# Sliding-window attention and a multiplicative feed-forward on one core: the first phase laid out anew

## The chip, the core and the metric

The kernel runs on one core of one Trainium2 chip. The core has five engines with instruction queues of their own: TensorE (PE, matrix products; PEld is its loading of weights), VectorE (DVE), ScalarE (ACT), GpSimd (POOL) and SyncE (SP). Transfers are issued by an engine's queue and carried out by 16 DMA engines. The metric is the time of one execution on the device in microseconds (us); less is better.

## What is computed

```python
# q, k, v: (8 batches, 8 heads, 576 tokens, 64); w1, w2: (512, 1024); w3: (1024, 1024); w_out: (1024, 512)
scores = scale * np.matmul(q, k.transpose(0, 1, 3, 2))
mask = (rel >= 0) & (rel < 64)                 # a token sees itself and the 63 before it
attn = softmax(np.where(mask, scores, -1e9))
x = (attn @ v).transpose(0, 2, 1, 3).reshape(4608, 512)
out = ((x @ w1) * (x @ w2)) @ w3 @ w_out       # float32, (4608, 512)
```

Inputs and output are float32. The kernel multiplies in float16 and sums in float32.

## The kernel before

**The fold.** There is no nonlinearity between `w3` and `w_out`, so the kernel makes `wc = w3 @ w_out` once (1024 x 512, `wc_sb`) and uses that for all tokens. `w3` is taken in eight row blocks of 128. `fold_t(fc)` transposes block `fc` with eight TensorE instructions (L432) and copies it from PSUM to `w3T` (L434). `fold_mm(fc, c0, c1)` multiplies it with columns `c0:c1` of `w_out` in eight products (L439) and casts the result into `wc_sb` (L440). `load_w3(fc, n)` loads `n` row blocks (L425), `load_wo` a half of `w_out` (L410); both are issued by POOL, and cast from float32 to float16 on the way. `load_rows` and `cast_rows` (a block of `w3` loaded as float32, and then cast by an engine) are defined but not called. The blocks of `w3` lie in space that `ab` and `xT` use later. `load_rows` puts its block into the space of `w2_sb`.

**Attention.** A step `s` covers 256 tokens in four groups of 64. `scores(s)` makes 64 small products (L275) on 32 of the 128 rows at a time; `weigh(d)` takes exp on ScalarE (L284) and applies the band, either by one VectorE product with a mask (L288) or by two selects on POOL (L245, L247). A step that holds a batch's first group always goes to VectorE, whatever `weigh` is told. `values(s)` makes the sums (L301) and the weighted values (L307), and `norm(s)` divides: ln and exp on ScalarE (L317, L318), two VectorE products into `xT` (L320). `keep_sums(s)` stores the sums for a check at the end, by SP. Before that, `load_qk` loads Q or K of a batch in four POOL transfers, one for each pair of heads (L210), and `transposes` turns them in blocks of 32 x 32 on VectorE, one instruction for each half of the heads (L220). `load_v` loads V in blocks of 64 tokens (L230), and `copy_v` makes the shifted copies on VectorE (L236, L238).

**Feed-forward.** A group `g` is 512 tokens. `ffn_ab(g, fc)` makes one 128-column block of `x @ w1` and `x @ w2` with four products each (L367), copies the first by ScalarE (L370) and multiplies on VectorE (L371). `ffn_o(g, t)` makes one output tile of 128 tokens with eight products (L383), and copies it out of PSUM (L385) for `store()`, which hands it to SP (L392). `ffn_ab` can also take two column blocks for half of the tokens (`nf`, `lo`, `hi`); before, no call does. The PSUM tiles of all of these but attention come from one ring of four (`f_ps`), those of attention from a ring of two (`a_ps`).

**Order.** Nothing is scheduled by a planner here (`tc.manual_schedule()`): each engine runs its instructions in the order of the calls in the text, and the framework adds the semaphore waits. POOL has at most eight transfers under way: each new one waits for the one eight before it to land. The text has two parts. The first phase, written out call by call, holds the fold, steps 0 to 6 of attention and groups 0 and 1. It is followed by a loop over groups 2 to 8, where `tick` interleaves attention steps at fixed places. `keep_busy(n)` makes `n` dummy products of the identity (L464).

The first phase of before begins so:

```python
load_qk(0, 'q')
make_identity(nc, ident16)
load_qk(0, 'k')
keep_busy(140)
load_w3(2, 2)
transposes(0, 'k', 1)
...
load_w3(0, 2)
load_wo(0, 256)
fold_t(0, act_cp)
fold_t(2, act_cp)
load_wo(256, 512)
```

Of the kernel before, what the change touches and what calls it, by code (L numbers as in the profile page):

```python
# [9 lines left out]
FP16 = mybir.dt.float16  # L10
I32 = mybir.dt.int32
# [4 lines left out]
P = 128  # L16
# [123 lines left out]
def kernel(  # L140
# [64 lines left out]
    def load_qk(b, which, *js):  # L205

        src = k if which == "k" else q
        r = RUN[b]
        for j in js or range(NJ):
            nc.gpsimd.dma_start(  # L210
                out=t16_of(b, which)[32 * j:32 * j + 32].rearrange("p hh (i n) -> p (hh i) n", n=r * D),
                in_=src[b, 2 * j:2 * j + 2].rearrange("hh (i p r) d -> p (hh i) (r d)", p=32, r=r))

    def transposes(b, which, hh):

        dst = kTs if which == "k" else qTs
        r = RUN[b]
        if b not in dst:
            dst[b] = sb.tile([P, 2, S, 2], FP16, name=which + "T")
        nc.vector.transpose(  # L220
            dst[b][:, hh].rearrange("q t c -> q (t c)").bitcast(I32).rearrange("q (i p r) -> q i r p", p=32, r=r),
            t16s[which, b][:, hh].bitcast(I32).rearrange("p (i r e) -> p i r e", r=r, e=32))
# [9 lines left out]
    def copy_v(b, half, i0, i1):  # L232

        vh = v16s[b % 3].rearrange("p (i o) h d -> p i o (h d)", o=2)
        if half == 0:
            dve_cp(vh[0:D, i0:i1, 1], vh[D:P, i0:i1, 0])  # L236
        else:
            dve_cp(vh[D:P, i0:i1, 1], vh[0:D, i0 + 1:i1 + 1, 0])  # L238
# [135 lines left out]
    def ffn_o(g, t, cp=dve_cp):  # L374
# [5 lines left out]
        for c0, c1, cp in halves:  # L380
# [4 lines left out]
            cp(o_sb[:, c0:c1], o_ps[:, 0:c1 - c0])  # L385
            stores.append((r0, c0, c1, o_sb))

    def store():
        while stores:
            r0, c0, c1, o_sb = stores.pop(0)  # L390
            queue = nc.scalar if c1 - c0 < DM and c0 == 0 else nc.sync
            queue.dma_start(out=out[r0:r0 + P, c0:c1], in_=o_sb[:, c0:c1])  # L392
# [34 lines left out]
    def fold_t(fc, cp):  # L427
# [5 lines left out]
        w3Ts[fc] = sb.tile([P, 8, P], FP16, name="w3T", bufs=4)  # L433
# [40 lines left out]
    load_qk(0, 'q')  # L474
    make_identity(nc, ident16)
    load_qk(0, 'k')
    keep_busy(140)
    load_w3(2, 2)
    transposes(0, 'k', 1)
    transposes(0, 'k', 0)  # L480
    transposes(0, 'q', 0)
    make_ones(nc.vector)
    load_w3(0, 2)
    load_wo(0, 256)
    fold_t(0, act_cp)
    fold_t(2, act_cp)
    load_wo(256, 512)
    transposes(0, 'q', 1)
    load_w3(4, 2)
    fold_t(1, dve_cp)  # L490
    load_v(0, 0, 2, 4)
    fold_t(3, dve_cp)
    make_band()
    load_v(0, 6, 7)
    scores(0)
    load_w3(6, 2)
    load_w12(1, 0, 512)
    fold_mm(3, 0, 256, dve_cp)
    fold_mm(0, 0, 256, act_cp)
    fold_mm(1, 0, 256, dve_cp)  # L500
    load_w12(0, 0, 512)
    weigh(0, nc.vector)
    weigh(1, nc.gpsimd)
    fold_mm(2, 0, 256, dve_cp)
    load_w12(0, 512, 1024)
    fold_mm(0, 256, DM, act_cp)
    fold_mm(2, 256, DM, dve_cp)
    fold_mm(1, 256, DM, act_cp)
    fold_t(4, dve_cp)
    copy_v(0, 0, 0, 2)  # L510
    copy_v(0, 1, 0, 2)
    fold_t(5, act_cp)
    copy_v(0, 0, 2, 4)
    scores(1)
    weigh(2, nc.vector)
    weigh(3, nc.gpsimd)
    fold_mm(4, 0, DM, act_cp)
    fold_mm(3, 256, DM, act_cp)
    load_qk(1, 'k')
    copy_v(0, 1, 2, 3)  # L520
    values(0)
    norm(0)
    load_w12(1, 512, 1024)
    fold_mm(5, 0, DM, dve_cp)
    fold_t(6, act_cp)
    load_qk(1, 'q')
    fold_t(7, dve_cp)
    values(1)
    norm(1)
    fold_mm(6, 0, DM, dve_cp)  # L530
    fold_mm(7, 0, DM, act_cp)
    ffn_ab(0, 2)
    ffn_ab(0, 0)
    ffn_ab(0, 1)
    transposes(1, 'k', 0)
    keep_sums(0)
    load_v(1, 0, 2, 4, 6, 7)
    load_qk(2, 'k')
    transposes(1, 'k', 1)
    ffn_ab(0, 3)  # L540
    ffn_ab(0, 5)
    ffn_ab(0, 4)
    transposes(1, 'q', 0)
# [3 lines left out]
    copy_v(1, 1, 0, 3)  # L547
    copy_v(1, 0, 0, 4)
    scores(2)
    weigh(4, nc.vector)  # L550
    weigh(5, nc.gpsimd)
    ffn_o(0, 0, act_cp)
    load_qk(2, 'q')
    scores(3)
    weigh(7, nc.vector)
    store()
    keep_sums(1)
    ffn_o(0, 1, dve_cp)
    load_v(2, 6, 7)
    weigh(6, nc.gpsimd)  # L560
    values(2)
    norm(2)
    load_v(2, 0, 2, 4)
    store()
    load_qk(3, 'q')
    ffn_o(0, 2, act_cp)
    values(3)
    transposes(2, 'k', 0)
    store()
    norm(3)  # L570
    transposes(2, 'k', 1)
    transposes(2, 'q', 0)
    ffn_o(0, 3, act_cp)
    ffn_ab(1, 0)
    store()
    ffn_ab(1, 1)
    load_qk(3, 'k')
    transposes(2, 'q', 1)
    ffn_ab(1, 2)
    copy_v(2, 0, 0, 4)  # L580
    ffn_ab(1, 3)
    scores(4)
    keep_sums(2)
    weigh(8, nc.vector)
    ffn_ab(1, 4)
    keep_sums(3)
    weigh(9, nc.gpsimd)
    store()
    store()
    store()  # L590
    ffn_ab(1, 5)
    transposes(3, 'q', 1)
    copy_v(2, 1, 0, 3)
    transposes(3, 'q', 0)
    load_v(3, 0, 2, 4)
    load_v(3, 6, 7)
    scores(5)
    weigh(10, nc.gpsimd)
    weigh(11, nc.gpsimd)
    ffn_ab(1, 6)  # L600
    ffn_ab(1, 7)
    values(4)
    store()
    store()
    transposes(3, 'k', 0)
    norm(4)
    store()
    transposes(3, 'k', 1)
    ffn_o(1, 0, act_cp)
    store()  # L610
    load_qk(4, 'k')
    load_qk(4, 'q')
    ffn_o(1, 1, act_cp)
    load_v(4, 0, 2, 4)
    store()
    copy_v(3, 0, 0, 4)
    scores(6)
    weigh(12, nc.vector)
    weigh(13, nc.vector)
    ffn_o(1, 2, dve_cp)  # L620
    keep_sums(4)
    values(5)
    norm(5)
    store()
    load_v(4, 6, 7)
    ffn_o(1, 3, dve_cp)
    copy_v(3, 1, 0, 3)
    keep_sums(5)
# [63 lines left out]
```

## Time and profile before

| | us |
|---|---|
| median of three runs | 259.8 (259.2 to 261.9) |
| the profiled execution | 260.8 |
| its span, first to last instruction | 259.1 |
| TensorE busy | 245.3 |
| of that, dummy products (L464) | 10.2 |

A profile is one execution. In the page's 40 slices a digit is the busy share in tenths, and one slice is 6.5 us. In a row of the timeline stand the start, the time taken, the engine, line and operation, output and input, the count and, in brackets, how long the engine had been idle and what ended that. Rows merge instructions of one kind. The largest groups are the products of the feed-forward:

```profile
L367 PE MATMUL f_ps<-xT,w_sb 128*128 128x512 f16 x576 | 129.6, 379 | 1.1 <-DVE t2k L385 1.1
L383 PE MATMUL f_ps<-wc_sb,ab 128*128 128x512 f16 (+1 forms) x296 | 65.6, 374 | 0.0
```

The first number behind the bar is the time that the group covers, the second the mean of one instruction in ns; products overlap, so 576 of 379 ns cover 129.6 us.

### The profile page before, as it was taken

The numbers are of one execution on the slowest core, as the hardware profiler recorded it, in microseconds if no ns is written. First come the engines' busy times: TensorE is split into PE (matmuls) and PEld (weight loads), VectorE is DVE, ScalarE is ACT, GpSimd is POOL, SyncE is SP. The second block draws the span as 40 slices with busy tenths as digits, with TensorE's granted clock in tenths as the row PEclk, the third lists the DMA queues.
The fourth block names the chain that finished last, engine by engine and source line by source line (L and its number), as shares of the span: only waits on it lengthen the run. The fifth ranks groups of instructions, "written<-read, shape, count | busy, mean of one in ns | idle before, by whom it ended". The sixth has DMA issues, their size and how long they took to land.

```text
span 259.1 us, 8273 instructions
## 1 busy us (share of the span) xinstructions
PE 245.3 (95%) x3622; PEld 129.8 (50%) x3622; DVE 145.8 (56%) x215; ACT 116.3 (45%) x174; POOL 114.3 (44%) x154
## 2 busy tenths in 40 slices
PE   2959999999999899999999999999999999999992
PEld 2958654454445345544444444444554444444441
DVE  0065664887877746656755776576466344434421
ACT  1024744276385464546545453654465545234210
POOL 7962867659669678593089018003000303003000
PEclk9999999999999999999999999999999999999999
DMA  5999999999994999599449909900300120022022
GB/s 80 170 201 189 194 205 206 155 198 149 186 159 53 188 203 150 83 140 213 53 66 219 157 0 128 132 5 13 152 3 5 71 100 1 3 81 85 1 79 89
DMA packets 75497, 29.57 MB, mean 114 GB/s; under 512 B 62456, under 2 KB 69880, under 8 KB 75456
## 3 DMA queue, kind: packets, MB, share of 16 engines
q0 software_dynamic: 69984, 19.41, 73.6%
q1 hardware_dynamic: 5328, 9.46, 9.9%
q8 instruction: 29, 0.48, 0.8%
q10 hardware_dynamic: 144, 0.13, 0.1%
q14 instruction: 12, 0.10, 0.1%
HBM read 38.80 MB, written 9.44 MB: 186 GB/s over the span
## 4 chain that ended last, share of the span: by engine, by line
PE 89%; DMA 4%; POOL 2%; ACT 1%; DVE 1%; issue 1%; POOLq 0%
PE f_ps L367 49%; PE f_ps L383 23%; PE f_ps L439 6%; PE a_ps L275 4%; DMA ab<-in_moe_w_dram 4%; PE a_ps L307 3%; PE a_ps L301 2%; PE f_ps L432 1%; POOL k L210 1%; POOL q L210 1%; ACT pt L284 1%; DVE w3T L434 1%; DVE t2k L385 0%; DVE xT L320 0%; POOL ab L425 0%
## 5 line engine op out<-in xcount | busy, mean ns | idle before, releaser
L367 PE MATMUL f_ps<-xT,w_sb 128*128 128x512 f16 x576 | 129.6, 379 | 1.1 <-DVE t2k L385 1.1
L367 PEld LDWEIGHTS <-w_sb 128*128 128x128 f16 x576 | 54.7, 98 | 65.8 <-issue 2.2
L371 DVE TENSOR_TENSOR ab<-f_ps,a_sb 128x512 f16<-128x512 f32 x72 | 49.7, 690 | 41.6 <-PE f_ps L367 39.6
L383 PE MATMUL f_ps<-wc_sb,ab 128*128 128x512 f16 (+1 forms) x296 | 65.6, 374 | 0.0
L370 ACT COPY a_sb<-f_ps 128x512 f32<-128x512 f32 x72 | 42.3, 587 | 48.6 <-PE f_ps L367 48.6
L245 POOL TENSOR_SCALAR_AFFINE_SELECT pt<-pt 128x1024 f16<-128x1024 f16 x11 | 12.6, 1144 | 80.8 <-ACT pt L284 80.7
L383 PEld LDWEIGHTS <-ab 128*128 128x128 f16 x296 | 27.9, 98 | 31.0
L284 ACT ACTIVATE pt<-a_ps 128x1024 f16<-128x1024 f32 x36 | 36.3, 1026 | 13.3 <-PE a_ps L275 13.2
L320 DVE TENSOR_TENSOR xT<-a_ps,r 128x512 f16<-128x512 f32 x36 | 23.2, 687 | 25.7 <-ACT r L318 25.7
L230 POOL DMA_DIRECT2D v<-in_v_dram x40 | 34.0, 863 | 7.1 <-DMA k<-in_k_dram 3.5
L385 ACT COPY t2k<-f_ps 128x512 f32<-128x512 f32 (+1 forms) x19 | 10.9, 575 | 42.3 <-PE f_ps L383 42.3
L288 DVE TENSOR_TENSOR pt<-pt,band 128x1024 f16<-128x1024 f16 x25 | 17.2, 693 | 14.1 <-ACT pt L284 14.0
L210 POOL DMA_DIRECT2D q<-in_q_dram x32 | 20.0, 638 | 4.8 <-DMA w_sb<-in_moe_w_dram 1.4
L220 DVE STREAM_TRANSPOSE kT<-k 128x576 int32<-128x576 int32 x16 | 14.7, 936 | 12.5 <-DMA k<-in_k_dram 12.5
L210 POOL DMA_DIRECT2D k<-in_k_dram x32 | 20.0, 645 | 2.8 <-DMA q<-in_q_dram 0.8
L385 DVE COPY t2k<-f_ps 128x512 f32<-128x512 f32 (+1 forms) x18 | 12.1, 673 | 7.9 <-PE f_ps L383 7.8
L439 PE MATMUL f_ps<-ab,w3T 128*128 128x256 f16 (+1 forms) x96 | 14.6, 308 | 0.3 <-DVE w3T L434 0.3
L220 DVE STREAM_TRANSPOSE qT<-q 128x576 int32<-128x576 int32 x16 | 14.6, 930 | 0.0
L464 PE MATMUL f_ps<-ident 128*128 128x128 f16 x140 | 10.2, 249 | 4.6 <-POOL ident masks.py:199 4.6
L307 PE MATMUL a_ps<-pt,v 128*32 128x64 f16 x1152 | 14.0, 193 | 0.0
L275 PEld LDWEIGHTS <-kT 32*128 32x128 f16 x1152 | 10.4, 92 | 7.2 <-issue 7.0
L317 ACT ACTIVATE ln_s<-a_ps 128x512 f32<-128x512 f32 x18 | 10.8, 597 | 7.2 <-PE a_ps L301 7.2
(43 smaller groups left out, 135.2 us busy)
## 6 DMA issues: line engine op xcount, KB each, us to landing
out_dram<-t2k SPq DMA_DIRECT2D x35, 256.0 KB, 2.5
q<-in_q_dram POOLq DMA_DIRECT2D x32, 144.0 KB, 6.8
k<-in_k_dram POOLq DMA_DIRECT2D x32, 144.0 KB, 7.4
v<-in_v_dram POOLq DMA_DIRECT2D x32, 128.0 KB, 6.1
w_sb<-in_moe_w_dram POOLq DMA_DIRECT2D x8, 256.0 KB, 9.0
ab<-in_moe_w_dram POOLq DMA_DIRECT2D x2, 512.0 KB, 9.1
ab<-in_moe_w_out_dram POOLq DMA_DIRECT2D x2, 512.0 KB, 12.8
xT<-in_moe_w_dram POOLq DMA_DIRECT2D x2, 512.0 KB, 14.1
```

The lines of the kernel that those rows point to most:

```text
L210: nc.gpsimd.dma_start(out=t16_of(b, which)[32 * j:32 * j + 32].rearrange("p hh (i n) -> p (hh i) n", n=r * D), in_=src[b, 2 * j:2 * j + 2] ...
L220: nc.vector.transpose(dst[b][:, hh].rearrange("q t c -> q (t c)").bitcast(I32).rearrange("q (i p r) -> q i r p", p=32, r=r), t16s[which, b ...
L230: nc.gpsimd.dma_start(out=vh[lo:P, c], in_=v[b, :, s0:s0 + P - lo, :].rearrange("h s d -> s h d"))
L284: nc.scalar.activation(pt, held.pop(d).rearrange("k j (a n) -> k (j a) n", a=2), AF.Exp, bias=-SHIFT, scale=scale)
L307: nc.tensor.matmul(o_ps[jp][32 * h:32 * h + 32, 0, o0:o0 + 64], v16s[b % 3][:, max(0, t - 1), 4 * jp + h, x:D:2], pt[:, h, 64 * i:64 * i + ...
L320: nc.vector.tensor_tensor(xT[:, 2 * jp:2 * jp + 2, x0:x0 + W], o_ps[jp][:, 0].rearrange("p (x n) -> p x n", x=2), r[:, jp].unsqueeze(1).br ...
L367: nc.tensor.matmul(d[:, f * n:f * n + n], w[:, dc, (fc + f) * P:(fc + f + 1) * P], xT[:, dc, x0:x0 + n], start=(dc == 0), stop=(dc == 3), ...
L370: act_cp(a_sb[:, 0:nf * n], a_ps[:, 0:nf * n])
L371: nc.vector.tensor_tensor(ab[:, fc:fc + nf, lo:hi], b_ps[:, 0:nf * n].rearrange("p (f n) -> p f n", f=nf), a_sb[:, 0:nf * n].rearrange("p ...
L383: nc.tensor.matmul(o_ps[:, 0:c1 - c0], ab[:, fc, t * P:t * P + P], wc_sb[:, fc, c0:c1], start=(fc == 0), stop=(fc == 7))
L385: cp(o_sb[:, c0:c1], o_ps[:, 0:c1 - c0])
L439: nc.tensor.matmul(o_ps[:, c0:c1], w3Ts[fc][:, ec, :], wo16[:, ec, c0:c1], start=(ec == 0), stop=(ec == 7))
```

## The change

- Two row blocks of `w3` (0 and 1) are loaded as float32 by SP, and cast by VectorE (three halves) and ScalarE (one). POOL's first loads are half of `w_out` and `w3` blocks 2 and 3, and Q and K of batch 0 come behind the rest of `w_out`.
- In batches with nine tokens to a partition (0 to 2), `load_qk` takes its four parts by half of the tokens and half of the heads, and `transposes` can take one half of the tokens. Batch 0 uses that.
- `w1` and `w2` come as two quarters and a half each. `ffn_ab` for the first four column blocks of group 0 runs in four calls of two blocks and 256 tokens.
- The fold's products all run in halves of 256 columns, `w3T` has eight buffers, and 30 and 20 dummy products take the place of 140.
- The rest of the first phase is reordered. Its last part now has `values(5)` and `norm(5)` ahead of three of the four `ffn_o` of group 1. V block 7 of batch 0 is loaded behind K of batch 2.
- The second half of the very last tile is copied in two pieces, by ScalarE and VectorE, and stored in two.

The loop over groups 2 to 8 is as before.

```diff
-    def load_qk(b, which, *js):
+    def load_qk(b, which, *parts):
...
+        for c in parts or range(4):
+            if r == 9:
+                i, hh = divmod(c, 2)
+                nc.gpsimd.dma_start(
+                    out=t16[:, hh, r * D * i:r * D * (i + 1)],
+                    in_=src[b, hh:H:2, 32 * r * i:32 * r * (i + 1)].rearrange("j (p r) d -> j p (r d)", r=r))
...
-    def transposes(b, which, hh):
+    def transposes(b, which, hh, *halves):
...
+        for t0, t1 in [(S // 2 * i, S // 2 * (i + 1)) for i in halves] or [(0, S)]:
...
+            if c0 == 0:
+                cp(o_sb[:, c0:c1], o_ps[:, 0:c1 - c0])
+                stores.append((r0, c0, c1, o_sb))
+            else:
+                for h0, h1, hcp in ((c0, 384, act_cp), (384, DM, dve_cp)):
+                    hcp(o_sb[:, h0:h1], o_ps[:, h0 - c0:h1 - c0])
+                    stores.append((r0, h0, h1, o_sb))
...
-            queue = nc.scalar if c1 - c0 < DM and c0 == 0 else nc.sync
+            queue = nc.scalar if c1 - c0 < DM and c1 < DM else nc.sync
...
-        w3Ts[fc] = sb.tile([P, 8, P], FP16, name="w3T", bufs=4)
+        w3Ts[fc] = sb.tile([P, 8, P], FP16, name="w3T", bufs=8)
```

The first phase of the changed kernel, up to the end of group 0's `ffn_ab`:

```python
load_rows(0, nc.sync)
load_wo(0, 256)
load_w3(2, 2)
make_identity(nc, ident16)
cast_rows(0, 0, dve_cp)
make_band()
load_w3(4, 2)
keep_busy(30)
load_wo(256, 512)
load_qk(0, 'k', 1); load_qk(0, 'k', 0); load_qk(0, 'q', 1); load_qk(0, 'q', 0)
load_rows(1, nc.sync)
cast_rows(1, 0, dve_cp); cast_rows(0, 1, dve_cp)
fold_t(0, dve_cp); fold_t(2, act_cp)
load_v(0, 0); load_w3(6, 2); load_v(0, 6); load_v(0, 2); load_qk(0, 'k', 2)
cast_rows(1, 1, act_cp)
load_qk(0, 'q', 2)
fold_mm(0, 0, 256, dve_cp)
load_qk(0, 'k', 3); load_w12(0, 256, 512)
fold_t(1, dve_cp)
load_v(0, 4)
fold_t(4, act_cp)
load_qk(0, 'q', 3)
fold_t(5, act_cp)
keep_busy(20)
load_w12(0, 0, 256)
make_ones(nc.vector)
fold_t(3, dve_cp)
transposes(0, 'k', 1, 0)
fold_mm(1, 0, 256, dve_cp)
load_w12(1, 0, 256); load_w12(1, 256, 512); load_qk(1, 'k')
load_w12(0, 512, 1024); load_w12(1, 512, 1024); load_qk(1, 'q')
transposes(0, 'k', 0, 0)
fold_mm(2, 256, DM, act_cp)
transposes(0, 'q', 0, 0); transposes(0, 'q', 1, 0)
fold_mm(3, 256, DM, dve_cp); fold_mm(4, 0, 256, act_cp)
fold_mm(5, 0, 256, act_cp); fold_mm(3, 0, 256, dve_cp)
copy_v(0, 0, 0, 1)
scores(0)
...
scores(1)
weigh(2, nc.vector)
fold_mm(7, 0, 256, act_cp)
copy_v(0, 1, 1, 3)
weigh(3, nc.vector)
ffn_ab(0, 0, 2, 0, 256)
values(1)
norm(1)
keep_sums(0)
fold_mm(4, 256, DM, act_cp)
ffn_ab(0, 2, 2, 0, 256)
load_qk(2, 'k')
transposes(1, 'k', 1)
ffn_ab(0, 0, 2, 256, 512)
ffn_ab(0, 2, 2, 256, 512)
load_v(0, 7)
transposes(1, 'k', 0)
ffn_ab(0, 5)
...
```

And its end, ahead of the loop:

```python
ffn_ab(1, 7)
store()
values(4); norm(4)
load_v(4, 6, 7)
ffn_o(1, 0, act_cp)
transposes(3, 'k', 0)
load_qk(4, 'k'); load_v(4, 0, 2, 4)
store()
values(5); norm(5); keep_sums(4)
ffn_o(1, 1, act_cp)
store()
transposes(3, 'k', 1)
ffn_o(1, 2, dve_cp)
keep_sums(5)
scores(6)
store()
copy_v(3, 0, 0, 4); copy_v(3, 1, 0, 3)
weigh(13, nc.vector); weigh(12, nc.gpsimd)
ffn_o(1, 3, act_cp)
```

More of the change, by code (lines that the diff above doesn't have):

```diff
@@ L514 @@
+    fold_t(7, dve_cp)
+    transposes(0, 'k', 0, 1)
+    values(0)
+    transposes(0, 'k', 1, 1)
+    load_v(1, 0, 2)
+    transposes(0, 'q', 0, 1)
+    norm(0)
+    transposes(0, 'q', 1, 1)
+    load_v(1, 4, 6, 7)
+    fold_mm(7, 256, DM, act_cp)
+    fold_mm(2, 0, 256, dve_cp)
+    fold_mm(6, 0, 256, act_cp)
+    copy_v(0, 0, 3, 4)
+    fold_mm(6, 256, DM, act_cp)
+    copy_v(0, 0, 1, 3)
     scores(1)
     weigh(2, nc.vector)
[L516 to L518 removed]
```

215 lines of the change are left out of this document (103 added, 112 removed).

## The prediction

> **What bounds the kernel now.** I read the page first: shares, then the 40 slices.
>
> ```profile
> PE 245.3 (95%) x3622; PEld 129.8 (50%) x3622; DVE 145.8 (56%) x215; ACT 116.3 (45%) x174; POOL 114.3 (44%) x154
> PE   2959999999999899999999999999999999999992
> DMA  5999999999994999599449909900300120022022
> ```
>
> TensorE is full in nearly every slice, but slices 0 to 2 (a slice is 6.5 us) hold dummy products, and there the DMA engines are full instead. So the trace's start comes next: three rows of the timeline, then the busy time by stage (busy us of PE, weight loads, VectorE, ScalarE and POOL with their instructions, the clock, the DMA share, and GB/s).
>
> ```profile
> 1.49 2.44 POOL L210 DMA_DIRECT2D q<-in_q_dram  x4 [0.96 <-POOLq L676]
> 4.57 10.20 PE L464 MATMUL f_ps<-ident 128*128 128x128 f16 x140 [4.57 <-POOL ident masks.py:199]
> 17.37 1.96 PE L432 MATMUL f_ps<-ident,ab 128*128 128x128 f16 x32 [2.60 <-DMA ab<-in_moe_w_dram]
> ...
> 3.20:12.40 9.20, 7.83 (x101) 7.84 (x102) 0.00 (x0) 0.00 (x0) 8.66 (x15) 1.00 1.07 161
> 12.40:45.60 33.20, 30.28 (x508) 21.02 (x506) 20.05 (x30) 14.92 (x22) 20.77 (x31) 1.00 1.37 199
> 17.37:53.06 35.69, 35.37 (x560) 22.34 (x561) 21.96 (x33) 17.27 (x26) 22.12 (x33) 1.00 1.48 190
> 53.06:89.87 36.81, 35.67 (x683) 17.58 (x675) 28.58 (x41) 21.95 (x31) 27.95 (x35) 1.00 1.36 154
> ```
>
> The 140 products of line 464 are dummies. Useful work begins at 17.37 us, when the first rows of w3 land behind all of Q and K of batch 0. From there to 53.06 TensorE is busy 35.37 of 35.69 us, and 35.67 of 36.81 up to 89.87. So time can be won in three places alone: before 17.37, in the one gap that the last stretch hides, and after the last product. DMA begins at 3.2 us (slice 0 is half full, and the first stage is cut there) and moves 161 GB/s at first, then 199. Transfers, not engines, decide when the weights are there.
>
> **Step 1: useful work starts earlier.** The first work that has to wait for much is now the transpose of rows 2 (`fold_t(2)`). Ahead of it stand two rows of w3 as fp32 by SP, half of w_out and one pair of w3. The sizes are in the page's list of DMA issues, SP's rate in its list of queues.
>
> ```profile
> q1 hardware_dynamic: 5328, 9.46, 9.9%
> ...
> q<-in_q_dram POOLq DMA_DIRECT2D x32, 144.0 KB, 6.8
> v<-in_v_dram POOLq DMA_DIRECT2D x32, 128.0 KB, 6.1
> w_sb<-in_moe_w_dram POOLq DMA_DIRECT2D x8, 256.0 KB, 9.0
> ab<-in_moe_w_dram POOLq DMA_DIRECT2D x2, 512.0 KB, 9.1
> ab<-in_moe_w_out_dram POOLq DMA_DIRECT2D x2, 512.0 KB, 12.8
> ```
>
> The fp32 rows are a kind of load that before doesn't have. SP's queue moved 9.46 MB of stores in 9.9% of the span, 25.7 us, so 369 GB/s; 1.05 MB then takes 2.8 us. The other two are 512 KB each, 1.05 MB: 5.3 us at 199 GB/s, 6.5 at 161. The first bytes of before came at 3.2 us, 1.7 after POOL began to issue; SP's may come at 2.0. Sum: 10.1 to 12.5 us; I take 11.3. By the Trainium skill (DMA: Bandwidth & Descriptors, Issuing engines are not separate DMA queues) a transfer from SP runs on the same 16 engines and saves issue time alone. No run here shows SP and POOL loading together, and the sum above adds the two transfers rather than overlapping them, as that rule would.
>
> The four casts (three on VectorE, one on ScalarE) have no row. A 256-column copy took 423 ns and a 1024-column fp16 one 686 (quoted below), so 0.3 to 0.7 us each: VectorE is through by about 8 us, hidden by the wait for rows 2. Without that cover they would cost 1.5 us. The identity was ready at 4.57 behind four issues (2.44 us in all); now two stand ahead of it. `make_band` stands in POOL's queue next, ahead of the third load:
>
> ```profile
> 14.27 0.66 POOL L245 TENSOR_SCALAR_AFFINE_SELECT band<-band 128x512 f16<-128x512 f16 x1
> ```
>
> That is the largest of its five instructions, so 3.3 us at most: the third load is issued by 7.9, while the two before it are under way to 11.3. No loss. Two waits are new: w2's pieces wait on POOL for the casts, which read the fp32 rows out of w2's buffer, and everything POOL issues later queues behind that. The last cast stands behind one ScalarE copy after rows 2, so it is done near 13, and POOL comes there after 20: nothing. SP has nothing else until the first `keep_sums`.
>
> **Step 2: TensorE's work up to `ffn_ab(0, 5)`, the first block that needs the upper half of w1 and w2.**
>
> ```profile
> 20.27 6.29 PE f_ps L439 x56
> 26.55 0.89 PE f_ps L432 x16
> ...
> 30.77 0.22 PE a_ps L301 x4
> 30.99 0.24 PE a_ps L307 x32
> 31.23 0.11 PE a_ps L301 x4
> ...
> 38.70 13.81 PE f_ps L367 x64
> 52.51 0.70 PE a_ps L275 x62
> ...
> L434 DVE COPY w3T<-f_ps 128x1024 f16<-128x1024 f16 x4 | 2.7, 686 | 2.9 <-PE f_ps L432 2.9
> L440 DVE CAST wc_sb<-f_ps 128x256 f16<-128x256 f32 x4 | 1.7, 423 | 2.7 <-PE f_ps L439 2.7
> ```
>
> The fence has pieces of the chain (start, us), then two groups by line. From 11.3: seven transposes of rows, 0.45 each (16 instructions in 0.89), 3.1; sixteen half products of the fold, 0.90 each (56 in 6.29, eight in one), 14.4; two scores, 0.70, 1.4; two values, 0.81 (0.22 + 0.24 and 0.11 + 0.24), 1.6; four half-token blocks of 16 products of 256 columns at 0.112, 7.2. Before did the same work with 512 columns, so splitting costs 0.3. Twenty dummies add 1.1. Together 28.8: 40.1 us at full clock.
>
> The clock is a term of its own, for the 140 dummies shrink to 30.
>
> ```profile
> 5.00:9.00 4.00, 4.00 (x40) 4.00 (x39) 1.00 1.04 148
> 10.00:14.00 4.00, 4.00 (x76) 4.00 (x74) 1.00 1.11 195
> ```
>
> These are the dummies alone: 40 in 4 us at first, 76 later, so TensorE ran at half speed for 4.4 us at least (to 9.0) and 5.4 at most; I use 4.7. If it does so again from 11.3, that loses 2.35; if the 30 dummies suffice, none. I take 1.2: 41.3.
>
> Do the data keep up? At 199 GB/s from 11.3: w3 rows 4 and 5 at 13.9, the rest of w_out 16.6, the first half of Q and K 19.5, its second half 29.1, the lower half of w1 and w2 33.0. TensorE comes to them at about 14, 17, 22, 31 and 32 to 36. Q and K still have to pass VectorE:
>
> ```profile
> 12.52 2.27 DVE L220 STREAM_TRANSPOSE kT<-k 128x576 int32<-128x576 int32 x2 [12.52 <-DMA k<-in_k_dram]
> ```
>
> Two whole ones in 2.27, so a half takes 0.57, and four stand in a row. VectorE is busy 22 of 36 us there, so it fits, with a margin of a microsecond. `weigh(3)` moves from POOL to VectorE, one multiplication of some 0.7 us; the deeper ring of transposed rows (8 for 4) costs no instruction.
>
> **Step 3: the upper half of w1 and w2.** Behind the lower half stand K of batch 1 (576 KB) and four weight pieces of 256 KB: 5.96 MB since 11.3. At 199 GB/s they are in at 41.3, at 190 (the row of 17.37 to 53.06) at 42.7. I take 42.7, the rate of the stretch with the same mix. It is later than TensorE's 41.3, so the weights decide. Four blocks follow at 1.73 (eight products each, 64 in 13.81) and one scores step, 0.70: 7.6, so 50.3 us. Before, the same point is 52.51 + 0.70 = 53.2. Gain 2.9.
>
> **Step 4: the gap before the regular phase.**
>
> ```profile
> 87.48 1.29 DVE L320 TENSOR_TENSOR xT<-a_ps,r 128x512 f16<-128x512 f32 x2 [0.35 <-ACT r L318]
> 88.22 0.59 PE L367 MATMUL f_ps<-xT,w_sb 128*128 128x512 f16 x2
> 88.68 0.68 DVE L385 COPY t2k<-f_ps 128x512 f32<-128x512 f32 x1
> 89.87 1.46 PE L367 MATMUL f_ps<-xT,w_sb 128*128 128x512 f16 x6 [1.06 <-DVE t2k L385]
> ```
>
> `values(5)` and `norm(5)` end just as block 0 of group 2 wants their output, one product group later. The change puts two output tiles, scores and a third tile in between, 3 x 1.8 + 0.7 = 6.1 us (a tile, like a block, is eight 512-column products), where ln, exp and two multiplications take 2.5. The idle 1.1 us goes. What is late next is `values(5)` itself, which waits for two selects on POOL:
>
> ```profile
> 74.57 0.61 PE a_ps L275 x61
> ...
> 79.87 1.15 POOL L247 TENSOR_SCALAR_AFFINE_SELECT pt<-pt 128x1024 f16<-128x1024 f16 x1
> ```
>
> Before, the second was done 5.8 us after its scores ended (81.0 against 75.2); now two blocks, `values(4)` and one tile lie between, 6.1 us. It just fits, so I count 1.1, between 0 and 1.2. The POOL queue in front of these selects holds only loads whose buffers come free in time. In phase 2 the other moves trade places among engines with a fifth or more of idle time: nothing. `load_v(0, 7)` now stands behind K of batch 2; by the same rate it lands near 53 (1.84 MB after 42.7: Q and V of batch 1, K of batch 2, the piece), and `values(2)` wants it near 55 (50.3, two tiles, one scores).
>
> **Step 5: the end.**
>
> ```profile
> 253.12 0.37 ACT L385 COPY t2k<-f_ps 128x256 f32<-128x256 f32 x1 [2.01 <-PE f_ps L383]
> 253.52 0.38 ACTq L392 DMA_DIRECT2D out_dram<-t2k  x1
> 253.99 0.42 DVE L385 COPY t2k<-f_ps 128x256 f32<-128x256 f32 x1 [1.05 <-PE f_ps L383]
> ```
>
> The last copy is halved over two engines, at most 0.2 less; but ScalarE's first store (253.52) now queues behind its second copy, and a second store of 0.38 behind it. Between -0.2 and +0.4; I take 0.
>
> **Sum.** 2.9 + 1.1 + 0 = 4.0 us. The profiled execution took 260.8 us with a span of 259.1: 256.8 and 255.1. The median of the three runs shown is 259.8, 1.0 lower than the profiled one: 255.8.
>
> **Rivals.** First: the transfers were the bound all along, and a new order moves no byte sooner.
>
> ```profile
> 37.69 0.70 POOL L405 DMA_DIRECT2D w_sb<-in_moe_w_dram  x1 [0.58 <-DMA w_sb<-in_moe_w_dram]
> ...
> DMA to landing us min/median/max: 7.7/9.0/10.6
> ```
>
> Before, the last weights landed at 37.69 + 7.7 = 45.4 at the earliest, with the same bytes ahead of them but 64 KB of V. At that pace the four blocks start at 45.1, the point is 52.7, the gain 0.5 + 1.1: 258.2. For it: DMA is full from 3.2 us on in both. Against: 161 GB/s was the rate for Q and K at the start, and SP starts sooner. With the gap moved rather than gone it is 259.3. Chance 0.23.
>
> Second, slower: the half clock stays. Before, it ended after 4.7 us without a break. Now 30 dummies and one transpose are followed by some 3 us of waiting for rows 2, and the work after them stops again for each load. If it stays at half speed up to `scores(0)`, 9.7 us of work takes 19.4; less the 1.2 counted and the 1.4 by which TensorE was early, +7.1: 262.9. It decides the sign once half speed lasts over 13 us or so after 11.3. Against it: from 11.3 there are no long gaps, and cold work fills them. The Trainium skill (TensorE: Matmul & The Clock Gate, Part 1) has the clock halved by an idle window of about 3.4 us and restored by a busy one; by that the loss would be 1.7 to 3.4 and this rival would fail. The trace agrees as far as its 4.7 us. Chance 0.12, and 0.05 for another new wait of that size.
>
> Third, better: loads run at 199 from 2.0 us and the clock is up. TensorE is ready at 38.9, the weights at 40.1, the point 47.7: 5.5 + 1.1 less, 253.2. Chance 0.12.
>
> **Numbers.** The forecast has 0.48: 255.8, on its own 254.5 to 257.2. The runs of before spread by 1% (259.2 to 261.9), so 1% (257.2 and 262.4) is about what a measurement can tell. Faster 0.60 (forecast and third), same 0.23, slower 0.17. The range leaves out the slow side and the end of the fast one: 253.2 to 260.5.
>
> **What would show it.** Right: first transposes of rows 2 at 10 to 12.5 us; `ffn_ab(0, 5)` starting at 41 to 44 after a wait for w2; ffn_o of group 0 near 50; no idle before group 2; the regular phase unchanged. Wrong: weights landing after 45, 128-column products at 107 ns beyond 20 us, `values` waiting for POOL, or a scores step waiting for VectorE's transposes.

## The result, and the profile after

The changed kernel takes 268.97 us (median of 6 runs, 268.1 to 271.49) against 260.74 of the kernel before on the same chip: ratio 1.034, 95% interval 1.0303 to 1.0377. It is slower by 8.2 us where 4 us less were forecast. The profiled execution took 268.31 us with a span of 266.6, 7.5 more than before. Medians take in every run of a kernel; the ratios leave out the few runs in a slower state (one each of a2, a4 and d1 below, two of d2, the profiled ones of d1 and d2 among them).

The slices of the page of after come first, then the one row of before that was not shown yet (GB/s in the same slices).

```profile
PE   4399988698999799999999999999999999999992
PEclk9769999999999799999999999999999999999999
DMA  6999999999999899949909971900220030022013
GB/s 185 199 181 146 165 127 163 176 131 141 209 195 157 89 183 197 91 79 201 153 1 148 212 73 44 204 6 2 81 82 1 27 138 5 1 81 80 2 57 108
```

```profile
GB/s 80 170 201 189 194 205 206 155 198 149 186 159 53 188 203 150 83 140 213 53 66 219 157 0 128 132 5 13 152 3 5 71 100 1 3 81 85 1 79 89
```

The DMA digits are nines in both, so by the busy share nothing has changed. The bytes have: 146, 165 and 127 GB/s in slices 3 to 5 (20 to 40 us), where before moved 189 to 205 (in 19 to 39). A busy DMA engine is not one that moves much. The same by stage, after first and then before (columns as in the prediction's stages; the last is GB/s):

```profile
18.00:24.00 6.00, 6.00 (x66) 5.36 (x64) 2.62 (x5) 1.71 (x4) 2.29 (x4) 1.00 1.92 162
24.00:36.00 12.00, 10.86 (x281) 8.93 (x279) 8.97 (x19) 6.12 (x12) 9.25 (x13) 1.00 1.45 155
36.00:44.00 8.00, 8.00 (x139) 7.03 (x137) 4.39 (x7) 5.24 (x9) 5.77 (x9) 1.00 1.04 119
```

```profile
18.00:24.00 6.00, 5.68 (x123) 5.09 (x121) 2.51 (x5) 3.70 (x5) 1.72 (x3) 1.00 1.37 202
24.00:36.00 12.00, 12.00 (x293) 8.74 (x291) 8.29 (x14) 8.09 (x13) 8.02 (x11) 1.00 1.56 191
36.00:44.00 8.00, 8.00 (x39) 3.64 (x38) 3.29 (x6) 2.54 (x5) 5.14 (x8) 1.00 1.23 204
```

From 18 to 44 us before moves 1212 + 2292 + 1632 KB (rate by length), 5.14 MB, and after 972 + 1860 + 952, 3.78 MB: 1.35 MB less, 6.8 us of transfers at 199 GB/s. Where TensorE pays for it stands in its timeline of after:

```profile
12.19 1.04 PE L447 MATMUL f_ps<-ident,ab 128*128 128x128 f16 x8 [4.43 <-DMA ab<-in_moe_w_dram]
...
46.41 0.61 PE L377 MATMUL f_ps<-xT,w_sb 128*128 128x512 f16 x2 [0.85 <-DMA w_sb<-in_moe_w_dram]
47.67 0.61 PE L377 MATMUL f_ps<-xT,w_sb 128*128 128x512 f16 x2 [0.65 <-DMA w_sb<-in_moe_w_dram]
48.96 0.60 PE L377 MATMUL f_ps<-xT,w_sb 128*128 128x512 f16 x2 [0.69 <-DMA w_sb<-in_moe_w_dram]
50.34 4.92 PE L377 MATMUL f_ps<-xT,w_sb 128*128 128x512 f16 x22 [0.77 <-DMA w_sb<-in_moe_w_dram]
...
56.54 0.68 PE L285 MATMUL a_ps<-qT,kT 32*128 32x64 f16 x64
...
63.10 0.42 PE L317 MATMUL a_ps<-pt,v 128*32 128x64 f16 x32 [1.11 <-DMA v<-in_v_dram]
...
89.12 0.40 PE L311 MATMUL a_ps<-pt,ones 128*32 128x256 f16 x4 [1.19 <-POOL pt L257]
...
98.92 0.68 PE L285 MATMUL a_ps<-qT,kT 32*128 32x64 f16 x64
```

Rows of w3 start the work at 12.19. Four times TensorE then waits for a piece of the upper halves of w1 and w2, from 45.6 (46.41 less 0.85) to 50.3; `values(2)` waits for V block 7, `values(5)` for POOL's selects. `scores(2)` starts at 56.54 and `scores(7)` at 98.92. In before they start thus:

```profile
52.45 0.68 PE L275 MATMUL a_ps<-qT,kT 32*128 32x64 f16 x64
...
91.26 0.68 PE L275 MATMUL a_ps<-qT,kT 32*128 32x64 f16 x64
```

So 4.1 us are lost by `scores(2)` and 3.6 more by `scores(7)`; from there on both kernels run alike (7.7 there, 7.5 at the end). Part of the 3.6 is the clock. It falls to half behind the wait for POOL, from 89.14 to 92.55 us by the trace's clock records (the 7 in slice 13 of PEclk), and 16 output products take 1.4 us longer there than later on:

```profile
89.95 4.86 PE f_ps L393 x16
...
113.44 3.45 PE f_ps L393 x16
```

The chain of waits of after names the transfers:

```profile
23.98 8.12 DMA k<-in_k_dram
...
36.20 9.39 DMA k<-in_k_dram
```

One load of 144 KB takes 9.39 us from issue to landing (the longest of any K load in before took 8.4), and POOL, which may have eight under way, stands behind it. That time counts the loads ahead as well, and so tells little by itself: b1 below, whose K loads have the form of before, has one of 10.4. The sign is the rate. These are the loads whose form the diff changed: 128 rows of SBUF at a time, four heads outermost at the source, where before had 32 rows of two heads.

### The profile page after: what moved, and what is told of

Read it like the earlier page. It is cut to its first block, busy times and chain, and to the rows that moved or that the text cites. A ratio compares the mean times of both kernels' runs of the same rounds, so it can differ in the third digit from the quotient of the medians.

```text
span 266.6 us, 8234 instructions
## 1 busy us (share of the span) xinstructions
PE 246.0 (92%) x3596; PEld 132.8 (50%) x3596; DVE 145.8 (55%) x223; ACT 118.6 (44%) x181; POOL 118.3 (44%) x155
## 4 chain that ended last, share of the span: by engine, by line
PE 65%; DMA 19%; POOL 12%; issue 2%; DVE 0%; ACT 0%; POOLq 0%
PE f_ps L377 37%; PE f_ps L393 21%; DMA k<-in_k_dram 12%; DMA v<-in_v_dram 7%; PE a_ps L285 3%; POOL v L240 3%; PE a_ps L317 2%; POOL q L213 2%; PE a_ps L311 2%; POOL pt L257 1%; POOL pt L255 1%; POOL q L217 1%; POOL w_sb L420 1%; POOL k L213 1%; POOL ab L425 1%
## 5 line engine op out<-in xcount | busy, mean ns | idle before, releaser
L377 PE MATMUL f_ps<-xT,w_sb 128*128 128x512 f16 (+1 forms) x608 | 130.5, 368 | 3.3 <-DMA w_sb<-in_moe_w_dram 3.0
L377 PEld LDWEIGHTS <-w_sb 128*128 128x128 f16 x608 | 57.5, 98 | 65.6 <-DMA w_sb<-in_moe_w_dram 4.7
L393 PE MATMUL f_ps<-wc_sb,ab 128*128 128x512 f16 (+1 forms) x296 | 67.1, 379 | 0.3 <-DVE ab L381 0.3
L240 POOL DMA_DIRECT2D v<-in_v_dram x40 | 34.1, 861 | 7.5 <-DMA ab<-in_moe_w_out_dram 2.4
L228 DVE STREAM_TRANSPOSE kT<-k 128x576 int32<-128x576 int32 (+1 forms) x18 | 15.4, 854 | 6.9 <-DMA k<-in_k_dram 6.9
L228 DVE STREAM_TRANSPOSE qT<-q 128x576 int32<-128x576 int32 (+1 forms) x18 | 15.1, 845 | 4.7 <-DMA q<-in_q_dram 4.7
L454 PE MATMUL f_ps<-ab,w3T 128*128 128x256 f16 x128 | 16.3, 282 | 0.2 <-issue 0.2
L396 DVE COPY t2k<-f_ps 128x512 f32<-128x512 f32 x16 | 11.0, 688 | 8.8 <-PE f_ps L393 8.8
L217 POOL DMA_DIRECT2D q<-in_q_dram x20 | 13.6, 683 | 4.6 <-DMA v<-in_v_dram 3.2
L317 PEld LDWEIGHTS <-v 128*32 128x32 f16 x1152 | 13.8, 98 | 1.5 <-DMA v<-in_v_dram 1.3
L217 POOL DMA_DIRECT2D k<-in_k_dram x20 | 13.3, 692 | 1.9 <-DMA v<-in_v_dram 1.1
```

Of the source, the lines that this page charges most:

```text
L217: nc.gpsimd.dma_start(out=t16[32 * c:32 * c + 32].rearrange("p hh (i n) -> p (hh i) n", n=r * D), in_=src[b, 2 * c:2 * c + 2].rearrange("h ...
L228: nc.vector.transpose(dst[b][:, hh, t0:t1].rearrange("q t c -> q (t c)").bitcast(I32) .rearrange("q (i p r) -> q i r p", p=32, r=r), t16s[ ...
L240: nc.gpsimd.dma_start(out=vh[lo:P, c], in_=v[b, :, s0:s0 + P - lo, :].rearrange("h s d -> s h d"))
L317: nc.tensor.matmul(o_ps[jp][32 * h:32 * h + 32, 0, o0:o0 + 64], v16s[b % 3][:, max(0, t - 1), 4 * jp + h, x:D:2], pt[:, h, 64 * i:64 * i + ...
L377: nc.tensor.matmul(d[:, f * n:f * n + n], w[:, dc, (fc + f) * P:(fc + f + 1) * P], xT[:, dc, x0:x0 + n], start=(dc == 0), stop=(dc == 3), ...
L393: nc.tensor.matmul(o_ps[:, 0:c1 - c0], ab[:, fc, t * P:t * P + P], wc_sb[:, fc, c0:c1], start=(fc == 0), stop=(fc == 7))
```

## The experiments

Times are medians, ratios against the kernel before on the same chip. The theory at first: the new form of the Q and K loads moves bytes more slowly. Rivals: the order, the cutting of w1 and w2, and the half clock.

**The load form in before alone** (a3). `load_qk` of before, with its loads for nine tokens to a partition in the new form:

```diff
+            if r == 9:
+                i, hh = divmod(c, 2)
+                nc.gpsimd.dma_start(out=t16[:, hh, r * D * i:r * D * (i + 1)], in_=...)
```

> The kernel before with the new load form for Q and K of batches 0 to 2 and nothing else of the change. Theory 'load form': some 9000 more 4-byte packets, the first rows of w3 land 2 to 6 us later than 17.37, time 263 to 268. Theories 'order' and 'clock': the form is free, 259 to 261.

Measured: 265.94 us, 1.0214 (1.0144 to 1.0285). With nothing else changed the form costs 5.3 us, as forecast (263 to 268).

**The form of before for batches 1 and 2** (a2; in the changed kernel, `if r == 9:` becomes `if parts:`).

> The changed kernel with the loads of before for Q and K of batches 1 and 2 alone; batch 0 keeps the new form. Theory 'load form': K of batch 1 gains about 4.5 us ahead of the upper weights, which land near 46; the first half of Q and K of batch 0 still takes 5.5 us; time 260 to 263. Theory 'order' and theory 'clock': 267 to 269.

Measured: 265.02 us, 1.0222 (1.0136 to 1.0307): better than after by 4.0 us by the medians and 3.1 by the ratios. The time lies between the 260 to 263 that the theory of the form forecast and the 267 to 269 of the others.

**Batch 0 in halves too, on 32 rows at a time** (a1; 16 loads of 72 KB).

```diff
-            if r == 9:
-                i, hh = divmod(c, 2)
-                nc.gpsimd.dma_start(out=t16[:, hh, ...], ...)
+            if parts:
+                i, h = divmod(c, 2)
+                for j in (2 * h, 2 * h + 1):
+                    nc.gpsimd.dma_start(
+                        out=t16[32 * j:32 * j + 32, :, r * D * i:r * D * (i + 1)],
+                        in_=src[b, 2 * j:2 * j + 2, 32 * r * i:32 * r * (i + 1)].rearrange("hh (p r) d -> p hh (r d)", r=r))
```

> The changed kernel with all Q and K of batches 0 to 2 loaded in pieces of 32 partitions again (batch 0 still in halves by tokens, 16 loads of 72 KB for 8 of 144 KB; batches 1 and 2 in the four loads of before). Theory 'load form' (the new loads, 128 partitions with an outermost count of four in the source, run on four of the 16 DMA engines): the 24 loads lose their extra 4-byte packets (11152 falls to about 2000), four loads of K of batch 1 take about 3 us instead of 7.7, the upper half of w2 lands at 43 to 45 instead of 50.3, and the time is 256 to 260. Theory 'order' (K of batch 1 stands ahead of the upper half of w1 and w2, and the bytes are what they are): w2 still lands near 50, time 267 to 269. Theory 'clock' (half speed from 10.6 to 17.5 us): no change of the first phase, 268.

Measured: 270.02 us, 1.0395 (1.0303 to 1.0486). A miss, and no clean test. The waits from 10 to 55 us show a new one:

```profile
DVE kT L229 <- DMA w_sb<-in_moe_w_dram: 9.9, 1, 9.9
```

VectorE's first-half transposes stood for 9.9 us, until 29.09. The view names a weight load, but in the trace the last of the second halves of K had landed just before, at 28.80. They are loads into the same tile, and stand ahead of these transposes in the text, so it is likely that the first halves waited for the second. With buffers of their own (f1, below) the longest such wait is 0.9 us.

**The order: upper halves of w1 and w2 ahead of K of batch 1** (a4).

> The changed kernel, its load form too, with the four loads of the upper half of w1 and w2 moved ahead of K of batch 1. Theory 'load form': w2 lands near 43, TensorE's wait of some 5 us before column block 5 goes, but K, Q and V of batches 1 and 2 come as late as before, so part of it comes back as a wait before scores of batch 1 or its values: 265 to 268. Theory 'order': the wait goes and stays away, 261 to 264. Theory 'clock': 268.

Measured: 269.03 us, 1.0369 (1.0284 to 1.0454), as after. Two rows of the chain, and one of VectorE's timeline:

```profile
43.16 7.57 DMA q<-in_q_dram
...
50.74 3.38 PE f_ps L377 x8
```

```profile
48.97 1.20 DVE L228 STREAM_TRANSPOSE kT<-k 128x576 int32<-128x576 int32 x1 [6.35 <-DMA k<-in_k_dram]
```

The last weights land at 45.7 now, 4.6 us earlier, and TensorE still gets on at 50.7. The chain names a load of Q, but the semaphore on which TensorE waits in the trace is VectorE's. VectorE stands 6.35 us for K of batch 1, with the multiplications of `ffn_ab` behind that transpose, and these free the PSUM tiles that TensorE needs. This order only chooses which transfer is waited for, and the order theory falls (it forecast 261 to 264).

**The form and the cutting of w1 and w2.** Three kernels: all of Q and K in the form of before, batch 0 whole in place of its first halves (b2); with it the lower w1 and w2 in four loads of 256 KB (b1); that alone (b3).

```diff
-    load_qk(0, 'k', 1); load_qk(0, 'k', 0); load_qk(0, 'q', 1); load_qk(0, 'q', 0)
+    load_qk(0, 'k'); load_qk(0, 'q')          # parts 2 and 3 drop out
...
-    load_w12(0, 256, 512)                      # b1 and b3
+    load_w12(0, 0, 512)
```

> The changed kernel with all Q and K in the four loads of before, and nothing else. Theory 'load form and issue': about half of the way, the upper w2 at 44 to 46, 258 to 262 us. Theory 'form alone': 256 to 259. Theory 'new order': 263 or more.

> The changed kernel with all Q and K in the four loads of before (32 partitions each; batch 0 whole, where its first halves stood) and the lower columns of w1 and w2 in four loads of 256 KB instead of eight of 128 KB. Theory 'load form and issue' (128-partition loads use four of 16 DMA engines, and small loads are bound by POOL's 0.7 us for each issue, 128 KB in 0.72 us being 180 GB/s at best): about 200 GB/s from 10 to 45 us, first half of Q and K there by 23, the upper half of w2 by 43 to 44, 256 to 259 us. Theory 'form alone': the same as the run with the load form alone, within 1 us. Theory 'new order is worse by itself': 263 or more.

> The changed kernel with the lower columns of w1 and w2 in four loads of 256 KB, the load form of Q and K as changed. Theory 'load form and issue': four issues of 0.72 us fewer, the upper w2 lands 1 to 3 us earlier than 50.3, 265 to 267 us. Theory 'form alone': no change, 268 to 269.

Measured: b2 259.12 us, 0.9953 (0.9913 to 0.9992); b1 258.71, 0.9939 (0.9904 to 0.9975); b3 264.68, 1.0159 (1.0084 to 1.0234). Mending the loads of Q and K alone takes 9.9 us off after, and the kernel is then a little faster than before. That takes back two things, the form of 24 loads and the halves of batch 0. By a2, the form of the 16 loads of batches 1 and 2 makes up 3 to 4 us of it (2 to 3 in d1, below); no run tells the form from the halving in the eight loads of batch 0. The cutting of w1 and w2 is worth 4.3 us while the slow loads stay, and 0.4, which is nothing, once they are gone; why it is so much beside the slow loads was not settled. That b1 and b2 lie within 1 us is what the theory of the form alone forecast; what b3 gains is not. The stages of b1, and its TensorE timeline:

```profile
18.00:24.00 6.00, 5.79 (x58) 5.07 (x56) 2.23 (x4) 1.62 (x4) 5.27 (x8) 1.00 1.36 198
24.00:36.00 12.00, 10.82 (x285) 9.46 (x285) 9.27 (x20) 7.10 (x12) 6.58 (x11) 1.00 1.48 195
36.00:44.00 8.00, 8.00 (x138) 6.95 (x136) 5.98 (x9) 4.45 (x9) 5.56 (x9) 1.00 1.23 203
```

```profile
24.91 0.24 PE L279 MATMUL a_ps<-qT,kT 32*128 32x64 f16 x8 [1.11 <-DVE qT L222]
...
39.24 12.31 PE L371 MATMUL f_ps<-xT,w_sb 128*128 128x256 f16 x80
51.48 0.68 PE L279 MATMUL a_ps<-qT,kT 32*128 32x64 f16 x64
```

The rate is 195 to 203 GB/s again, and no wait for weights is left: 80 products run from 39.24 without a break.

**The form back in b1, for batches 1 and 2 only** (d1; `if r == 9 and b:` with the new form).

> The changed kernel with Q and K of batch 0 in the four loads of before and the lower halves of w1 and w2 in four loads (258.7 us), but with the new load form put back for batches 1 and 2 (16 loads). If a load of the new form runs on 4 of the 16 DMA engines, each of the 16 leaves 12 engines with 32 packets of 4 bytes, so 6,144 more small packets than the same kernel without it; K of batch 1 takes 6 us or more for its 590 KB instead of some 3, the upper halves of w1 and w2 land at 46 to 48 instead of 43.5, and the time is 261.5 to 263. If only the splitting of batch 0 by tokens was to blame, the time stays at 258.5 to 259.

Measured: 261.59 us, 1.0016 (0.9986 to 1.0046): 2.9 us slower than b1 by the medians, 2.0 by the ratios. The time is as forecast, but not the wait: in this trace the last weights land at 46.7, and TensorE waits for none of them. It stands for 1.4 us at 39.2 instead, at a place that the clock experiments below explain. The packet rows of the pages, b1 and then this kernel:

```profile
DMA packets 75657, 30.09 MB, mean 117 GB/s; under 512 B 62488, under 2 KB 70040, under 8 KB 75616
```

```profile
DMA packets 81801, 30.12 MB, mean 114 GB/s; under 512 B 68632, under 2 KB 76184, under 8 KB 81760
```

The difference is 6144 small packets, exactly 384 for each of the 16 loads, as expected. The Trainium skill (DMA: Bandwidth & Descriptors, Why a DMA increments its semaphore by 16 and not by 1) says that a DMA runs on the largest number of engines up to 16 that divides the outermost size on both sides, and notes an exception for some copies from this queue; four heads outermost make that 4 engines. The trace agrees. 384 is 12 by 32, as if each of 12 idle engines got 32 packets. And the trace keeps the 16 semaphore updates by which each load reports its end. Of the four loads of K of batch 1 in after, the first has 12 of them early (from 37.1 us), the next 8, then 4, then none, and the others follow from 40.5 to 45.8. K and Q of batch 0 (first halves) and K of batch 1 in d1 show the same 12, 8, 4 and 0. In b1 the 16 updates of each load of K of batch 1 come within 1.9 us. This is what loads on four engines each would give, the next load on the next four. Four such loads together then reach all 16, and yet the rate falls; why that is so stays open.

**Halves by tokens in the good form, in buffers of their own.** The loads of a1 into two tiles for each of Q and K (f1); the same with w1 and w2 as in b1 (f2).

```diff
-                        out=t16[32 * j:32 * j + 32, :, r * D * i:r * D * (i + 1)],
+                        out=half_of(which, i)[32 * j:32 * j + 32],
```

> The changed kernel with all that it does, batch 0 in halves by tokens included, but every load of Q and K on 32 partitions at a time: the halves of batch 0 are 16 loads of 72 KB into buffers of their own, batches 1 and 2 are loaded as before. If the load form was the whole loss, the upper halves of w1 and w2 land at 43 to 45 us, scores(0) starts before 24.5, and the time is 257.5 to 259.5. If the number of loads on POOL's queue limits (16 of some 0.55 us for 1.18 MB), the upper halves land after 46 and the time is 261 to 265.

> The same with the lower halves of w1 and w2 in four loads of 256 KB instead of eight of 128 KB. If the number of loads limits, it is 1 to 4 us faster than the one beside it; if not, within 0.7 us of it.

Measured: f1 264.19 us, 1.0146 (1.0089 to 1.0203); f2 265.93, 1.0189 (1.0131 to 1.0247). f1's stages, its row of the loads (ns: least, median, most), its chain, and TensorE's waits at the start of `scores(1)` (us in all, how many, the longest):

```profile
18.00:24.00 6.00, 6.00 (x69) 5.50 (x67) 3.52 (x7) 2.08 (x5) 5.75 (x9) 1.00 1.08 127
24.00:36.00 12.00, 9.49 (x213) 7.90 (x211) 4.86 (x10) 5.91 (x11) 8.34 (x13) 1.00 1.24 137
36.00:44.00 8.00, 6.14 (x163) 4.78 (x163) 5.58 (x11) 3.23 (x5) 7.23 (x13) 0.79 1.22 169
```

```profile
L221 POOL DMA_DIRECT2D k16h<-in_k_dram x8: 535/548/595, 8.0 to 27.1; - x8
```

```profile
31.36 4.07 DMA q16h<-in_q_dram
...
36.40 1.26 DVE xT L338 x2
37.66 0.60 DVE qT L236
...
38.31 0.94 PE a_ps L293 x51
```

```profile
PE a_ps L293 <- DVE xT L338: 3.6, 2, 3.2
```

POOL needs 0.55 us to issue a load of 72 KB (0.55 to 0.82 for 144 KB in before). 72 KB in 0.55 us is 134 GB/s, close to the 127 to 137 measured. From 18 to 24 us POOL is busy for 5.75 of 6.00 us, which bears that out; from 24 to 36 for 8.34 of 12.00, so there the issues are not the whole limit. The halves do bring `scores(0)` forward (24.4 us in f1 and 23.0 in f2, against 24.9 in b1 after its wait), but the second halves land near 35, and `scores(1)` waits for them, 3.2 us at a stretch in f1 and 4.3 in f2. Behind this wait the clock falls: 0.79 from 36 to 44 us in f1 and 0.62 in f2, where b1 has 1.00. Waits and clock together come to about what f1 and f2 lose against b1 by `scores(2)`, 5.4 and 5.5 us. f2, with four loads fewer, did not gain the 1 to 4 us that the theory of the issues forecast, though it moves 150 and 165 GB/s in the first two stages. So the splitting costs in either form, by loads on few engines or by many small ones; how much of the late second halves is the issuing is not shown.

**The clock.** b1 with 50 more full dummy products ahead of `fold_t(2)` (b4), and without its 30 and 20 (d2):

> As the first of these four, with 50 more dummy products behind the first transpose of w3, where TensorE waits from 7.5 to 12 us. Theory 'clock' as a part: full speed from 12 us on, TensorE about 2 to 2.5 us earlier at scores 0, and as much off the time only where the weights are not what ends last: 0 to 2.5 us less than without the dummies. If the weights decide, no difference.

> The same 258.7 us kernel without any dummy products (30 and 20 taken out). If the half clock costs time at the end (the second rival), half speed lasts longer than to 17.5 us and the time rises by 1 to 3 us. If the arrival of the data sets the end of the first phase, the time stays within 0.5 us of 258.7, and could fall by that much because the 20 dummies (1.1 us) go.

Measured: b4 261.32 us, 1.0033 (1.0 to 1.0066); d2 261.51, 1.0036 (1.0002 to 1.007). More dummies and fewer both lose against b1, 2.6 and 2.8 us by the medians and 2.4 and 2.5 by the ratios. The clock alone cannot do that. The chain of b4 has two pauses in which TensorE waits for nothing:

```profile
30.64 1.04 issue
31.67 0.41 PE a_ps L311 x30
...
36.30 0.32 PE f_ps L448 x2
36.62 1.54 issue
```

Each follows a 16 KB transfer on the instruction queue. These are from the packets, instructions and chains of the traces of b4, d2 and two kernels below, in us (the profiled execution of b4 took 263.2, above its median; how often both pauses come is open). The last column counts the instructions of TensorE, products and weight loads, that the trace has ahead of the pause:

```
kernel   transfer        TensorE goes on   of that a pause of   instructions ahead
b4       29.22 to 30.17  31.67             1.04                  705
b4       35.66 to 36.60  38.16             1.54                  961
d2       34.36 to 35.31  36.97             0.53                  705
d2       40.97 to 41.92  43.28             1.53                  961
e2       29.36 to 30.31  31.80             0.11                  705
e2       35.54 to 36.65  38.02             1.26                  961
e1       35.47 to 36.44  37.86             0.66                 1217
```

705, 961 and 1217 are 256 apart. e1, which has 256 instructions more than b1 (128 dummies, each with its weight load), also has one 16 KB transfer more (30 against 29), so 256 instructions make one such block. The pauses stand a whole number of blocks apart, whatever the instructions there do, and end 1.4 to 1.7 us after the next block has landed. The pause of d1 at 39.2 has 961 ahead of it too. In b1 the blocks land at 30.33 and 36.30, and TensorE comes to the borders at 32.64 and 37.81, late enough to wait 0.2 us at most.

The next theory was that instructions come late, and that dummies move the places at which the 16 KB blocks end. Three kernels test it with short dummies (32 x 32): b4 with 78 of them, which makes a full block more than b1 (e1); b1 with 50 (e2); d2 with 50 at the start, which brings the block ends back to where b1 has them (e3).

```diff
+            nc.tensor.matmul(d, ident16[0:32, 0:32], ident16[0:32, 0:32], start=True, stop=True)
...
     fold_t(0, dve_cp)
+    keep_busy(50)          # e1 (and b4)
+    keep_short(78)         # e1; 50 in e2; in e3 50 ahead of fold_t(0)
```

> The kernel with 50 more full dummy products (261.3 us) and 78 short ones of 32 x 32 behind them, so that TensorE's queue holds 256 instructions, one 16 KB transfer of the instruction queue, more than in the 258.7 us kernel, and the borders of these transfers fall where they fall there. If the two pauses of 1.04 and 1.54 us with nothing to wait for came from late instructions, they go, and the time falls to 258.0 to 259.2; what is left against 258.7 is the clock's share. If they came from anything else that the dummies do, they stay, and the time is 261 or more.

> The 258.7 us kernel with 50 short dummy products of 32 x 32 alone, in a stretch where TensorE waits for a load. They take no heat to speak of, but move the borders by 100 instructions, as the 50 full ones did. Late instructions: pauses of 1 to 1.5 us appear at 30 to 32 and 36 to 39 us, and the time is 260.5 to 261.5. If the borders do not matter, the time stays at 258.7.

> The kernel without full dummy products (261.5 us) with 50 short ones at the start, so that the borders fall as in the 258.7 us kernel and the clock stays as it was without dummies. Late instructions: the pauses of 0.72 and 1.80 us go and the time falls to 259 to 260; what is left against 258.7 is the price of half speed at 26 to 30 us (some 1.9 us at most). If the clock was the whole cause, it stays at 261 to 261.5.

Measured: e1 259.03 us, 0.9946 (0.9918 to 0.9974); e2 261.51, 1.0043 (1.0017 to 1.0069); e3 259.88, 0.9972 (0.9941 to 1.0003). All three times fall where late instructions put them (e2 at the edge). Two details did not: e1 keeps one pause of 0.66, and in e2 only the second pause came in full. The rest of e2's loss is the clock, which dropped to half behind a wait of 2 us for Q. That stage in e2, and in b1, where the wait was shorter (the clock stands ahead of the DMA share):

```profile
25.90:29.30 3.40, 3.40 (x46) 2.52 (x35) 0.94 (x2) 2.23 (x3) 1.13 (x3) 0.58 1.74 185
```

```profile
25.90:29.30 3.40, 3.40 (x54) 3.09 (x41) 2.34 (x6) 3.18 (x5) 1.33 (x4) 1.00 1.64 189
```

**`values(5)` and `norm(5)` moved in before alone** (with `keep_sums(4)`, ahead of the second output tile of group 1), and **the last copy of before in b1**:

> The kernel before with one move alone: values(5), norm(5) and keep_sums(4) stand ahead of the second output tile of group 1 instead of behind the third. Prediction's step 4: the idle 1.06 us ahead of group 2 goes, and the time falls by 1.1 us (0 to 1.2). Rival: values(5) then waits for POOL's two selects and the gap has only moved, time unchanged.

> The 258.7 us kernel with the last copy and its store as before (one copy of 256 columns, two stores). Prediction's step 5: between 0.2 us slower and 0.4 us faster than 258.7. If the split of the last copy brought anything of note, it is slower by 0.5 us or more.

Measured: the move 260.31 us, 0.9985 (0.9954 to 1.0016), no difference that these runs can tell; the copy 259.29, 0.9945 (0.992 to 0.9971), 0.6 more than b1 by the medians and 0.2 by the ratios, within the spread of either. The timeline of the first shows part of the gap in a new place, where `scores(6)` waits for `norm(5)`:

```profile
84.83 0.67 PE L275 MATMUL a_ps<-qT,kT 32*128 32x64 f16 x62 [0.34 <-DVE xT L320]
...
90.72 0.68 PE L275 MATMUL a_ps<-qT,kT 32*128 32x64 f16 x64
```

`scores(7)` comes 0.54 us earlier than in before, not 1.1.

## Why the prediction was wrong

**Step 1 held.** Rows 2 were put at 11.3 (10.1 to 12.5), and their transposes began at 12.19. SP's and POOL's loads did run side by side (377 GB/s from 3 to 5 us, then 164 and 178 to 9 us), and adding them was near enough.

**Step 2's and 3's data failed, and with them the sign.** The sum let every byte move at 199 or 190 GB/s, whatever the form of its load. The diff gives Q and K another form, and that edit was costed at nothing; alone in before it costs 5.3 us. The first halves were put at 19.5 and the second at 29.1; they landed at 23.4 and 34.1. The upper halves of w1 and w2 were put at 42.7 and landed at 50.3. With the old loads in the same order (b1) the last piece lands at 43.5: the rate and the order were right, the form was not. Going back to the old loads, with batch 0 whole, takes 9.9 us off after, more than the whole loss of 8.2.

**Step 2's TensorE work was also too small.** In b1, which waits for no weights, the 48 half products left at 39.24 end near 44.5 (48 at 0.109), 3.2 us behind the 41.3 of the prediction: 0.8 from the start, some 1.7 from `scores(0)` waiting for VectorE's transposes of whole Q and K, and the rest mostly half clock beyond the 1.2 that the sum had for it. So even with the form mended, the first stage gains 1.0 us (51.48 against 52.45) and not 2.9. Bringing `scores(0)` forward needs the halves, and in both forms tried the halves cost more than they save.

**Step 3's chain** turned into waits: two that the prediction had named as signs of failure (weights after 45, `values(5)` on POOL) and V block 7, put at 53 and landed at 63.1. The clock, which the sum did not price after `scores(0)`, fell to half behind the wait for POOL.

**Step 4** had a margin of 0.3 us. In after it fails, since POOL's selects queue behind late loads; in b1 from `scores(2)` to `scores(7)` it is 37.74 us against 38.81, 1.07 less, as forecast. Alone in before it brought 0.54 us in the profiled execution, about half of that.

**Step 5** held: no difference that the runs can tell.

**The rivals.** The first, transfers as the bound, named the right resource, but with the rate unchanged, so it ended at 258.2. The second, half clock up to `scores(0)`, happened in part. In after the clock was half from 10.6 to 17.5 us:

```profile
10.70:17.40 6.70, 5.21 (x42) 4.71 (x43) 1.16 (x3) 2.25 (x3) 2.58 (x4) 0.50 1.28 196
```

It was not what made the time. With the clock full there (e1, 256-column products of 109 ns from 13.9 us, against 213 in b1) the kernel is no faster than b1: `scores(0)` waits for Q's transposes in both, and starts only 0.6 us earlier. A drop later, at 26 to 29 us, costs more (e3, without full dummies, against b1: 1.2 us by the medians, 0.9 by the ratios). The other side of the range was given to the wrong mechanism; none of the rivals had a slower load.

What stays open: why four loads on four engines each move fewer bytes than loads on 16, why the cutting of w1 and w2 matters only beside the slow loads, and whether some order makes the halves pay.

## What to carry to other kernels

A DMA whose pattern is rewritten is a new DMA, even where bytes and count are the same: before costing it, look at the outermost size on both sides, and afterwards at GB/s and small packets, not at the busy share. Cutting loads to bring the first piece forward has a floor, the issue time of the queue that sends them. An estimate from f1: 0.55 us at 199 GB/s is 110 KB, so while the queue does nothing but issue, smaller pieces move more slowly than the whole.

## What the hardware showed that was not expected

- Loads on few engines leave a mark in the packet row. By the reading above each puts 32 small packets on each of the other 12 engines: 9280 more in after than in b1, of which 24 loads by 384 are 9216.
- TensorE can wait for its own instructions. The Trainium skill (Runtime: NRT & Kernel Launch, Instruction fetch mechanics) has them fetched in 16 KiB blocks of 256 and calls the cost mostly hidden; in stretches of many small products with the DMA engines full, the traces show pauses of 0.5 to 1.5 us, each at a border between two such blocks. 50 idle-time dummies of 32 x 32 cost 2.8 us (e2), part of it this way. That TensorE waits there for the block to come is inferred from the places, from the 1.4 to 1.7 us behind each landing, and from the three runs that moved the borders.
- A wait shorter than the half clock that follows it can be enough. The trace's records have it at half for 3.41 us behind waits of 1.19 (after, 89.14 to 92.55, with 0.33 and 0.20 shortly before) and 1.68 us (e2, 25.34 to 28.75), and b1 kept the full clock behind one of 1.11. Where no record stands the column says 1.00: b1's first is at 16.37 us, and before that 256-column products take 213 ns. Their times tell.
